# SwiGLU's second block products three positions later, in an attention, MoE and SwiGLU kernel on one core

## The chip, the cores and the metric

The kernel runs on one core of one Trainium2 chip. The metric is the device time of one execution in microseconds (us). The kernel before was timed in three runs: 2015.36 us median, 2013.31 to 2016.67.

## The reference

Three layers follow one another on 2304 tokens of width 512:

```
attention:  q_s = softmax over head_dim, k_s = softmax over seq, kv = k_s^T v, out = q_s kv
MoE:        P = 8 Sinkhorn rounds on exp(x w_gate); out = sum over 8 experts P[:, e] * (relu(x w1[e]) w2[e])
SwiGLU:     xn = x / rms(x) * g;  out = (silu(xn w_gate) * (xn w_val)) w_out
```

The expert products are 512 x 1024 x 512 for each of 8 experts, the SwiGLU products 512 x 1536 (twice) and 1536 x 512.

## The kernel before

**Groups and units.** The tokens lie in three groups of 512, 896 and 896 columns (groups 0, 1, 2). The hidden width is cut into chunks of 256. A unit is one chunk of one group: units 0 to 95 are the MoE, units 96 to 113 the SwiGLU: 96 to 101 (group 1), 102 to 107 (group 2), 108 to 113 (group 0). `NU` is 96, `NC2` 6 and `U0` 108. Every fp32 product is made of three fp32r matmuls on a high and a low part (`mm3`, lines 107 to 109).

**Seven block products.** For groups 1 and 2 the products are Strassen's: `seven` (line 856 on) makes seven products of 128 x 448 blocks, of six matmuls each, for the gate (`"a"`), then seven for the value (`"v"`). So a unit of 96 to 107 has fourteen positions, 0 to 13. After each product ScalarE copies or VectorE combines its PSUM bank (L873, L887, L891, L900, L901); there are two banks `b1`, one `b2`, one `b3`, so a later product waits for a bank that VectorE has not yet read. Then `later(i)` runs: Silu on ScalarE at positions 5 and 7, and one y tile.

**y tiles.** The second product of the gated chunk is also cut in seven blocks of two tiles: 14 y tiles of three matmuls (`yo`), which run one at each position of the unit after their own (`YS`, `y_step`). Tile p needs block p // 2 of the gated values (`SB`), and a quarter of the out-weights, wo block p // 4 (`WO`, 512 KB each, `wo_load`, L1194). VectorE adds a tile to its place from PSUM (L1284), or, for the four numbers in `STAGED`, ScalarE copies it out (L1281) and GpSimd adds it (L1282).

**Steps that make the gated blocks.** `tail_steps` gives nine: value(0) and value(1), products of 896 columns on VectorE (L1216), and seven blocks, each a cast on ScalarE (L103) and a subtraction on VectorE (L104); four of the steps also subtract on GpSimd (L1212). Before, they run at positions 11, 12, 13 of their unit and ahead of y tiles 0 to 5 of the next.

**Group 2's norm.** During units 97 to 100 `spread` hands out 59 steps that normalize group 2, transpose it and make seven sums for each of two halves. A sum is a cast on ScalarE (L392), a subtraction on VectorE (L395) and a store of both parts (L405, `sdB`, `sdT`); a piece of the store lies in one of two buffers, so a cast waits for the store of two sums ago. Before, places are positions 0 to 13 with 8 and 10 twice (16 in a unit).

**Queues.** All loads and stores here go out on SyncE's one queue in the order of the program. In unit u the gate weights of u + 1 are loaded after position 6 and the value weights of u + 1 after position 13 (`ws_load`, L300, two loads of 128 x 1792 fp32, for unit 102's value weights after its position 0). In unit 101, after positions 7 to 13, the seven sums of group 2 come back (`sx_load`, L808, 128 x 1792 fp32 each), each when its predecessor of group 1 has been used last. Before, wo blocks 0 to 3 of unit u are loaded after positions 3, 7, 11 and 13 of u; of unit 101 blocks 2 and 3 after positions 1 and 2 of unit 102.

**Units 108 to 113** are plain: four runs of matmuls (`plain`, gate twice, value twice, each of four steps kk of three matmuls over 512 columns); the y tiles of unit 107 run between the steps in unit 108. `w2_split` (L104 with L103) makes the parts of the out-weights of unit u after hooks 0 and 1 of u and then loads the next (`w2_load`, L188). Hooks 0 and 1 stand ahead of the gate runs, 2 behind them, 3 and 4 ahead of the value runs, 5 behind them. `y_end` and `y_store` (L1298, L1309) add and write out groups 1 and 2.

Of the kernel before, what the change touches and what calls it, by code (L numbers as in the profile page):

```python
# [18 lines left out]
def kernel(  # L19
# [34 lines left out]
    KD = DM // P  # L54
# [11 lines left out]
    NC2 = FF // CH  # L66
    NU = NG * NCH
# [5 lines left out]
    U0 = NU + 2 * NC2  # L73
# [28 lines left out]
    def split(hi, lo, src, eng=None):  # L102
        nc.scalar.copy(hi, src)  # L103
        (eng or nc.vector).tensor_tensor(lo, src, hi.bitcast(F32), op=ALU.subtract)  # L104
# [18 lines left out]
    def bank(kind, cols, name):  # L123
        turn = BANK[kind]
        turn.append(turn.pop(0))
        pool = turn[-1]
        if isinstance(pool, str):
            return pb_tile(pool, name)[:, :cols]
        return pool.tile([P, cols], F32, tag="p", name=name)
# [61 lines left out]
    def w2_split(u, f):  # L191
        rv = RAW["b", u]
        if f == 0:
            W2[u] = tuple(
                w2p.tile([P, 2, DM], F32R, tag=f"w2{w}", name=f"w2{w}_{u}") for w in "hl"
            )
        g = group(u)[0]
        if u < NU and g == 2:

            nc.scalar.copy(W2[u][0][:, f], rv[:, f])  # L200
            if f == 0:
                nc.sync.dma_start(
                    W2[u][1].rearrange("p f d -> p (f d)").bitcast(F32), W2D.pop(u)
                )
        else:
            split(W2[u][0][:, f], W2[u][1][:, f], rv[:, f])
        if f == 1:
            if u < NU and g == 1:
                W2D[u + NCH] = dram.tile([P, 2 * DM], F32, tag=f"w2l{u}", name=f"w2d_{u}")
                nc.sync.dma_start(  # L210
                    W2D[u + NCH], W2[u][1].rearrange("p f d -> p (f d)").bitcast(F32)
                )
            del RAW["b", u]
            if u + 1 != NU and u + 1 < ALL:
                w2_load(u + 1)
# [692 lines left out]
    def group(u):  # L908
        if u < NU:
            return divmod(u, NCH)  # L910
        j, c = divmod(u - NU, NC2)
        return TURN2[j], c
# [10 lines left out]
    def plain(u, f, key, stored):  # L923

        ph = bank("h", 2 * GP[0], f"ph_{key[0]}_{u}_{f}")
        if YS:
            for kk in range(KD):
                plain_mm(ph, f, key, stored, (kk,))
                y_step()
        else:  # L930
            plain_mm(ph, f, key, stored, range(KD))
        return ph

    def plain_mm(ph, f, key, stored, kks):
        wh, wl = WS[key]
        xh, xl = X0
        for kk in kks:
            if stored:
                i = ((2, 3), (0, 1))[f][kk // 2]
                lh, ll = wh[:, i, kk % 2], wl[:, i, kk % 2]  # L940
            else:
                lh, ll = (plain_view(t)[:, kk, f * P:(f + 1) * P] for t in (wh, wl))
            mm3(ph, lh, ll, xh[:, kk], xl[:, kk], kk == 0, kk == KD - 1)
# [189 lines left out]
    def unit2_h(u, hook):  # L1133
        g, c = group(u)
        n = 2 * GP[g]

        def gate_part(cf, to):
            nc.scalar.activation(to, cf, AF.Silu)

        def value_part(cf, to, f):  # L1140
            nc.vector.tensor_tensor(to, cf, to, op=ALU.mult)
            split(*h_tiles(u, f), to)

        cg = cp_.tile([P, 2, 2, G], F32, tag="c", name=f"cg_{u}")
        if g == 0:
            for f in range(2):
                hook(f)
                to = cg[:, f].rearrange("p t g -> p (t g)")[:, :n]
                gate_part(plain(u, f, ("a", u), True), to)
            del WS["a", u]  # L1150
            hook(2)
            for f in range(2):
                hook(3 + f)
                to = cg[:, f].rearrange("p t g -> p (t g)")[:, :n]
                value_part(plain(u, f, ("v", u), True), to, f)
            del WS["v", u]
            hook(5)
            return
        flat = lambda t, f: t[:, f].rearrange("p t g -> p (t g)")
        cv = cp2.tile([P, 2, 2, G], F32, tag="cv", name=f"cv_{u}")  # L1160
        mine = tail_steps(u, cg, cv)

        def later(i):
            if i in (5, 7):
                gate_part(flat(cg, i // 7), flat(cg, i // 7))
            elif i >= 11:
                mine.pop(0)()
            y_step()
            hook(i)

        hook(-1)
        seven(("a", u), cg, later, lambda f: None)
        seven(("v", u), cv, lambda i: later(7 + i), lambda f: None)
        assert not YS
        YS.extend(y_steps(u, mine))

    YS = []
    YM = {}
    SB = {}
    WO = {}  # L1180
    STAGED = (2, 4, 12, 13)
    OT = ["pch", "pcl"]

    def y_step():
        if YS:
            YS.pop(0)()
# [12 lines left out]
    def block(u, i, src):  # L1199

        tag = "h" + "hl"[i % 2] + "01"[i // 2 % 2]
        t = hp_.tile([P, 2 * G], F32R, tag=tag, name=f"s_{u}_{i}").rearrange(
            "p (w n) -> p w n", w=2
        )
        SB[u, i] = t
        split(t[:, 0], t[:, 1], src)

    def tail_steps(u, cg, cv):

        t1 = cp2.tile([P, G], F32, tag="t1", name=f"t1_{u}")  # L1210
        b11, b12, b21, b22 = (cv[:, f, t] for f in range(2) for t in range(2))
        sub = lambda o, x, y: nc.gpsimd.tensor_tensor(o, x, y, op=ALU.subtract)  # L1212
        row = lambda t, f: t[:, f].rearrange("p t g -> p (t g)")

        def value(f):
            nc.vector.tensor_tensor(row(cv, f), row(cv, f), row(cg, f), op=ALU.mult)  # L1216

        def s0():
            sub(t1, b12, b11)
            block(u, 0, b11)  # L1220

        def s1():
            block(u, 1, t1)

        def s2():
            value(1)

        def s3():
            block(u, 2, b21)
            sub(t1, b22, t1)  # L1230

        def s4():
            block(u, 3, t1)
            sub(b21, b21, t1)

        def s5():
            block(u, 4, b22)
            sub(b12, b22, b12)

        return [lambda: value(0), s0, s1, s2, s3, s4, s5, lambda: block(u, 5, b21), lambda: block(u, 6, b12)]  # L1240

    def ym_place(g):

# [12 lines left out]
        four = [big[:, n * 2 * G:(n + 1) * 2 * G] for n in range(4)]  # L1256
        YM[g] = four[:3] + [more_[0], four[3], more_[1], more_[2]]

    def y_steps(u, more_):

        g, c = group(u)

        def tile_(p):
            i, m = divmod(p, 2)
            if p == 0 and c == 0:
                ym_place(g)
            if more_:
                more_.pop(0)()
            py = bank("y", G, f"yo_{u}_{p}")
            w = WO[u, i // 2][:, i % 2, :, m * P:(m + 1) * P]  # L1270
            x = SB[u, i]
            mm3(py, w[:, 0], w[:, 1], x[:, 0], x[:, 1], True, True)
            a = YM[g][i][:, m * G:(m + 1) * G]
            if c == 0:
                if p % 2:
                    nc.vector.tensor_copy(a, py)
                else:
                    nc.scalar.copy(a, py)
            elif p in STAGED:
                t = accp.tile([P, G], F32, tag="yt", name=f"yt_{u}_{p}", bufs=2)  # L1280
                nc.scalar.copy(t, py)  # L1281
                nc.gpsimd.tensor_tensor(a, t, a, op=ALU.add)  # L1282
            else:
                nc.vector.tensor_tensor(a, py, a, op=ALU.add)  # L1284

        return [lambda p=p: tile_(p) for p in range(14)]
# [110 lines left out]
    def task(kind, u, i, fn):  # L1397
        TASK.setdefault((kind, u, i), []).append(fn)
# [4 lines left out]
    for n, key in enumerate(keys):  # L1403
# [3 lines left out]
        kd, u = keys[n - 2]  # L1407
        i = 6 if kd == "a" else 13
        if u >= NU and group(u)[0] == 0:
            i = 2 if kd == "a" else 5  # L1410
        at = {("v", NU): ("y", NU - 2, 0), ("v", NU + NC2): ("h", NU + NC2, 0)}
# [10 lines left out]
            task("h", u, 1 + f, lambda u=u, f=f: w2_split(u, f))  # L1422
    for u in range(U0, ALL):
        for f in range(2):
            task("h", u, 5 if u == U0 else f, lambda u=u, f=f: w2_split(u, f))
    for u in range(NU, U0):
        for i in range(4):
            at = ("h", u, min(4 * i + 3, 13))
            if u == NU:
                at = ("h", u, i) if i < 2 else ("y", u - 1, 6)  # L1430
            elif u == NU + NC2 - 1 and i > 1:
                at = ("h", u + 1, i - 1)
            task(*at, lambda u=u, i=i: wo_load(u, i))
    for u in range(NCH, 2 * NCH):
        task("h", u - 2, 2, lambda u=u: ws_sums(u))
# [96 lines left out]
    for i in range(7):  # L1532
        task("h", NU - 1, i, lambda i=i: sx_load(NG + 1, i))
        task("h", NU + NC2 - 1, 7 + i, lambda i=i: sx_load(NG + 2, i))
    spread(
        [("h", u, i) for u in range(NU + 1, NU + NC2 - 1) for i in (*range(14), 8, 10)],
        lambda: norm_steps(2),
    )
    spread(
# [11 lines left out]
    with tc.manual_schedule():  # L1551
# [59 lines left out]
        for step in START.split():  # L1611
            op, i = step.split("-")
# [68 lines left out]
        at = LATE * CPE  # L1681
# [6 lines left out]
        while n < len(order):  # L1688
            kind, u = order[n]
# [68 lines left out]
```

## Time and profile before

| | us |
|---|---|
| median of three runs | 2015.36 |
| the profiled execution | 2016.0 |
| its span, first to last instruction | 2013.9 |
| TensorE busy in the span | 1984.6 |
| VectorE busy | 1479.8 |
| ScalarE busy | 826.5 |
| GpSimd busy | 492.2 |

The profiled execution is 0.6 us above the median, and 2.1 us of it lie outside the span. Matmuls overlap in the records: one of 448 columns is shown with some 0.36 us, while the next starts 0.2 us later, so lost time is read from the starts and not from busy time. Times in the trace count from the span's start. The SwiGLU's units 96 to 107 lie between 1582 and 1901 us, the plain units behind them.

### The profile page before, as it was taken

The numbers are of one execution on the slowest core, as the hardware profiler recorded it, in microseconds if no ns is written. First come the engines' busy times: TensorE is split into PE (matmuls) and PEld (weight loads), VectorE is DVE, ScalarE is ACT, GpSimd is POOL, SyncE is SP. The second block draws the span as 40 slices with busy tenths as digits, with TensorE's granted clock in tenths as the row PEclk, the third lists the DMA queues.
The fourth block names the chain that finished last, engine by engine and source line by source line (L and its number), as shares of the span: only waits on it lengthen the run. The fifth ranks groups of instructions, "written<-read, shape, count | busy, mean of one in ns | idle before, by whom it ended". The sixth has DMA issues, their size and how long they took to land.

```text
span 2013.9 us, 26582 instructions
## 1 busy us (share of the span) xinstructions
PE 1984.6 (99%) x9614; PEld 1715.8 (85%) x9614; DVE 1479.8 (73%) x2382; ACT 826.5 (41%) x1508; POOL 492.2 (24%) x438
## 2 busy tenths in 40 slices
PE   7999999999999999999999999999999999999999
PEld 5777888888888888888888888888888897899987
DVE  8885877676667777777658878888875459788864
ACT  5564433345343334433244343443332274444421
POOL 3330000032222222222013332333320025433400
PEclk8999999999999999999999999999999999999999
DMA  8543232354755566654778888888875758867644
GB/s 199 141 143 105 94 101 95 96 199 182 271 204 195 203 220 222 210 198 177 297 264 285 283 278 315 306 303 307 314 273 177 275 201 279 338 227 249 244 167 143
DMA packets 192259, 441.90 MB, mean 219 GB/s; under 512 B 33920, under 2 KB 101504, under 8 KB 191744
## 3 DMA queue, kind: packets, MB, share of 16 engines
q1 hardware_dynamic: 188432, 438.38, 63.0%
q10 hardware_dynamic: 3696, 1.84, 0.3%
q8 instruction: 75, 1.23, 0.3%
q14 instruction: 56, 0.46, 0.1%
HBM read 297.42 MB, written 142.74 MB: 219 GB/s over the span
## 4 chain that ended last, share of the span: by engine, by line
PE 93%; DVE 4%; DMA 2%; ACT 1%; issue 0%; SPq 0%; DVEq 0%; ACTq 0%
PE py L107 13%; PE py L108 13%; PE py L109 13%; PE b_a L109 10%; PE b_a L107 10%; PE b_a L108 10%; PE ph_a L107 3%; PE ph_a L109 3%; PE ph_a L108 3%; PE b_v L109 1%; PE b_v L107 1%; PE b_v L108 1%; PE yo L107 1%; PE yo L108 1%; PE yo L109 1%; DMA wsl_v<-wdl_v 1%
## 5 line engine op out<-in xcount | busy, mean ns | idle before, releaser
L107 PE MATMUL py<-w2h,hh 128*128 128x512 f32 x1152 | 452.6, 393 | 0.7 <-ACT lt L751 0.7
L108 PE MATMUL py<-w2l,hh 128*128 128x512 f32 x1152 | 449.0, 390 | 0.0
L109 PE MATMUL py<-w2h,hl 128*128 128x512 f32 x1152 | 448.7, 389 | 0.0
L873 ACT COPY u_a<-b_a 128x448 f32<-128x448 f32 x228 | 121.6, 533 | 605.5 <-PE b_a L109 599.1
L107 PEld LDWEIGHTS py<-w2h,hh 128*128 128x128 f32 x1152 | 216.3, 188 | 47.2 <-issue 1.5
L109 PEld LDWEIGHTS py<-w2h,hl 128*128 128x128 f32 x1152 | 216.3, 188 | 45.8
L108 PEld LDWEIGHTS py<-w2l,hh 128*128 128x128 f32 x1152 | 216.4, 188 | 42.9
L107 PE MATMUL b_a<-sT,wsh_a 128*128 128x448 f32 x608 | 221.0, 364 | 2.4 <-DVE c L887 1.2
L109 PE MATMUL b_a<-sT,wsl_a 128*128 128x448 f32 x608 | 220.6, 363 | 0.0
L108 PE MATMUL b_a<-sT,wsh_a 128*128 128x448 f32 x608 | 220.5, 363 | 0.0
L1013 DVE SCALAR_TENSOR_TENSOR slot_a<-py,Pm,slot_a 128x512 f32<-128x512 f32 x217 | 162.5, 749 | 52.4 <-PE py L109 50.3
L1013 DVE SCALAR_TENSOR_TENSOR slot_b<-py,Pm,slot_b 128x512 f32<-128x512 f32 x217 | 160.5, 744 | 19.5 <-PE py L109 18.9
L107 PE MATMUL b_a<-sB,wsh_a 128*128 128x448 f32 x456 | 165.6, 363 | 0.1
L109 PE MATMUL b_a<-sB,wsl_a 128*128 128x448 f32 x456 | 165.6, 363 | 0.0
L108 PE MATMUL b_a<-sB,wsh_a 128*128 128x448 f32 x456 | 165.4, 363 | 0.0
L249 POOL TENSOR_TENSOR sum<-w1r 128x256 f32<-128x256 f32 x32 | 23.7, 740 | 561.5 <-PE ph_a L109 244.1
L898 POOL TENSOR_TENSOR c<-u_a,p_a 128x448 f32<-128x448 f32 x64 | 74.1, 1158 | 328.0 <-ACT u_a L873 311.2
L947 DVE SCALAR_TENSOR_TENSOR hl<-c,hh 128x896 fp32r<-128x896 f32 x128 | 143.5, 1121 | 0.9 <-ACT hh L946 0.7
L104 DVE TENSOR_TENSOR w2l<-w2r,w2h 128x512 fp32r<-128x512 f32 x138 | 100.1, 726 | 50.6 <-ACT w2h L103 50.5
L946 ACT ACTIVATE hh<-c 128x896 fp32r<-128x896 f32 x128 | 122.3, 956 | 29.4 <-POOL c L898 27.8
L107 PEld LDWEIGHTS b_a<-sT,wsh_a 128*128 128x128 f32 x608 | 113.8, 187 | 13.8 <-DVE c L887 2.4
L897 DVE TENSOR_TENSOR c<-b_a,u_a 128x448 f32<-128x448 f32 x64 | 39.9, 624 | 114.1 <-ACT u_a L873 114.1
(275 smaller groups left out, 3913.4 us busy)
## 6 DMA issues: line engine op xcount, KB each, us to landing
w2r<-in_moe_w_dram SPq DMA_DIRECT2D x96, 512.0 KB
w1r<-in_moe_w_dram SPq DMA_DIRECT2D x64, 512.0 KB
wsdh<-wsh_a SPq DMA_DIRECT2D x32, 896.0 KB
wsdl<-wsl_a SPq DMA_DIRECT2D x32, 896.0 KB
wsh_a<-wsdh SPq DMA_DIRECT2D x32, 896.0 KB
wsl_a<-wsdl SPq DMA_DIRECT2D x32, 896.0 KB
wo<-wd_o SPq DMA_DIRECT2D x36, 512.0 KB
w2d<-w2l SPq DMA_DIRECT2D x32, 512.0 KB
```

Source lines behind the costliest of these rows:

```text
L104: (eng or nc.vector).tensor_tensor(lo, src, hi.bitcast(F32), op=ALU.subtract)
L107: nc.tensor.matmul(ps, lh, rh, start=first, stop=False, skip_group_check=True)
L108: nc.tensor.matmul(ps, lh, rl, start=False, stop=False, skip_group_check=True)
L109: nc.tensor.matmul(ps, ll, rh, start=False, stop=last, skip_group_check=True)
L249: nc.gpsimd.tensor_tensor(s1, a21, a22, op=ALU.add)
L873: nc.scalar.copy(tmp[n], bk[i])
L897: nc.vector.tensor_tensor(c[:, 1, 0], bk[2], tmp["u3"], op=ALU.add)
L898: nc.gpsimd.tensor_tensor(c[:, 1, 1], tmp["u3"], tmp["p5"], op=ALU.add)
L946: nc.scalar.activation(th, src, AF.Relu)
L947: return lambda: nc.vector.scalar_tensor_tensor(tl, src, 0.0, th.bitcast(F32), op0=ALU.max, op1=ALU.subtract)
L1013: nc.vector.scalar_tensor_tensor(a, py, pe, a, op0=ALU.mult, op1=ALU.add)
```

## The change

The y tiles run three positions later: `YS` is filled up with empty steps to three ahead of a unit's fourteen, so tile p of unit u comes at position p + 3 of unit u + 1, and tiles 11 to 13 at positions 0 to 2 of unit u + 2. In unit 102 positions 0 to 6 take two tiles each. The nine steps get positions of their own through a table `MORE`: 11, 12, 13 of their unit and 0, 1, 3, 5, 7, 8 of the next (for unit 101's: 0, 0, 1, 2, 3, 4), ahead of that position's y tile. `STAGED` becomes 3, 8, 10, 11. The wo blocks move to positions 6 and 10 of their unit and 0 and 2 of the next, with exceptions at the ends of the groups: blocks 1, 2, 3 of unit 101 come after positions 1, 2, 3 of unit 102. The norm steps of group 2 get 15 places in a unit. In the plain units the parts of the out-weights are made three hooks later.

```diff
--- before.py
+++ after.py
@@ -923,12 +923,12 @@
     def plain(u, f, key, stored):
 
         ph = bank("h", 2 * GP[0], f"ph_{key[0]}_{u}_{f}")
-        if YS:
-            for kk in range(KD):
-                plain_mm(ph, f, key, stored, (kk,))
-                y_step()
-        else:
-            plain_mm(ph, f, key, stored, range(KD))
+        for kk in range(KD):
+            plain_mm(ph, f, key, stored, (kk,))
+            at = KD * (2 * (key[0] == "v") + f) + kk
+            for fn in MORE.pop((u, at), ()):
+                fn()
+            y_step()
         return ph
 
     def plain_mm(ph, f, key, stored, kks):
@@ -1158,27 +1158,30 @@
             return
         flat = lambda t, f: t[:, f].rearrange("p t g -> p (t g)")
         cv = cp2.tile([P, 2, 2, G], F32, tag="cv", name=f"cv_{u}")
-        mine = tail_steps(u, cg, cv)
+        tail_steps(u, cg, cv)
 
         def later(i):
             if i in (5, 7):
                 gate_part(flat(cg, i // 7), flat(cg, i // 7))
-            elif i >= 11:
-                mine.pop(0)()
+            for fn in MORE.pop((u, i), ()):
+                fn()
             y_step()
+            if u == NU + NC2 and i < 7:
+                y_step()
             hook(i)
 
         hook(-1)
         seven(("a", u), cg, later, lambda f: None)
         seven(("v", u), cv, lambda i: later(7 + i), lambda f: None)
-        assert not YS
-        YS.extend(y_steps(u, mine))
+        YS.extend([lambda: None] * max(0, LAG - len(YS)) + y_steps(u))
 
     YS = []
     YM = {}
     SB = {}
     WO = {}
-    STAGED = (2, 4, 12, 13)
+    STAGED = (3, 8, 10, 11)
+    LAG = 3
+    MORE = {}
     OT = ["pch", "pcl"]
 
     def y_step():
@@ -1219,9 +1222,6 @@
             sub(t1, b12, b11)
             block(u, 0, b11)
 
-        def s1():
-            block(u, 1, t1)
-
         def s2():
             value(1)
 
@@ -1237,7 +1237,13 @@
             block(u, 4, b22)
             sub(b12, b22, b12)
 
-        return [lambda: value(0), s0, s1, s2, s3, s4, s5, lambda: block(u, 5, b21), lambda: block(u, 6, b12)]
+        for i, fn in (
+            (11, lambda: value(0)), (12, s0), (13, lambda: block(u, 1, t1)), (14, s2), (15, s3),
+            (17, s4), (19, s5), (21, lambda: block(u, 5, b21)), (22, lambda: block(u, 6, b12)),
+        ):
+            if u == NU + NC2 - 1 and i > 14:
+                i = {15: 14, 17: 15, 19: 16, 21: 17, 22: 18}[i]
+            MORE.setdefault((u + i // 14, i % 14), []).append(fn)
 
     def ym_place(g):
 
@@ -1256,7 +1262,7 @@
         four = [big[:, n * 2 * G:(n + 1) * 2 * G] for n in range(4)]
         YM[g] = four[:3] + [more_[0], four[3], more_[1], more_[2]]
 
-    def y_steps(u, more_):
+    def y_steps(u):
 
         g, c = group(u)
 
@@ -1264,8 +1270,6 @@
             i, m = divmod(p, 2)
             if p == 0 and c == 0:
                 ym_place(g)
-            if more_:
-                more_.pop(0)()
             py = bank("y", G, f"yo_{u}_{p}")
             w = WO[u, i // 2][:, i % 2, :, m * P:(m + 1) * P]
             x = SB[u, i]
@@ -1422,14 +1426,18 @@
             task("h", u, 1 + f, lambda u=u, f=f: w2_split(u, f))
     for u in range(U0, ALL):
         for f in range(2):
-            task("h", u, 5 if u == U0 else f, lambda u=u, f=f: w2_split(u, f))
+            task("h", u, 5 if u == U0 else 3 + f, lambda u=u, f=f: w2_split(u, f))
     for u in range(NU, U0):
         for i in range(4):
-            at = ("h", u, min(4 * i + 3, 13))
+            at = (("h", u, 6), ("h", u, 10), ("h", u + 1, 0), ("h", u + 1, 2))[i]
             if u == NU:
                 at = ("h", u, i) if i < 2 else ("y", u - 1, 6)
-            elif u == NU + NC2 - 1 and i > 1:
-                at = ("h", u + 1, i - 1)
+            elif u == NU + NC2 - 1 and i > 0:
+                at = ("h", u + 1, i)
+            elif u == NU + NC2:
+                at = ("h", u, 8 + i)
+            elif u == U0 - 1 and i > 1:
+                at = ("h", u + 1, 1)
             task(*at, lambda u=u, i=i: wo_load(u, i))
     for u in range(NCH, 2 * NCH):
         task("h", u - 2, 2, lambda u=u: ws_sums(u))
@@ -1533,7 +1541,8 @@
         task("h", NU - 1, i, lambda i=i: sx_load(NG + 1, i))
         task("h", NU + NC2 - 1, 7 + i, lambda i=i: sx_load(NG + 2, i))
     spread(
-        [("h", u, i) for u in range(NU + 1, NU + NC2 - 1) for i in (*range(14), 8, 10)],
+        [("h", u, i) for u in range(NU + 1, NU + NC2 - 1) 
+         for i in (0, 1, 2, 4, 6, 8, 8, 9, 9, 10, 10, 10, 12, 13, 13)],
         lambda: norm_steps(2),
     )
     spread(
```

## Rows read from the trace of the kernel before

**Rows 1.** The page, its first part: TensorE's and the other engines' busy time.

```profile
PE 1984.6 (99%) x9614; PEld 1715.8 (85%) x9614; DVE 1479.8 (73%) x2382; ACT 826.5 (41%) x1508; POOL 492.2 (24%) x438
```

**Rows 2.** Windows of units 99, 100, 101, 102, 103: stretch, length, each engine's busy time.

```profile
1662.40:1691.40 29.00, 26.62 (x127) 23.29 (x126) 24.83 (x35) 14.37 (x29) 14.88 (x11) 1.00 0.85 290
1691.40:1720.20 28.80, 26.66 (x127) 23.23 (x127) 26.96 (x34) 14.08 (x28) 16.89 (x13) 1.00 0.85 279
1720.20:1745.70 25.50, 25.50 (x127) 23.65 (x127) 18.93 (x27) 11.65 (x22) 11.04 (x9) 1.00 0.79 291
1745.70:1773.90 28.20, 26.44 (x128) 23.35 (x128) 18.92 (x27) 11.63 (x22) 10.69 (x9) 1.00 0.89 357
1773.90:1799.30 25.40, 25.40 (x128) 23.68 (x127) 22.40 (x29) 13.31 (x26) 7.19 (x6) 1.00 0.63 217
```

**Rows 3.** TensorE's waits from 1575 us on: total us, times, longest.

```profile
PE b_v L107 <- DVE cg L901: 2.6, 2, 1.5
PE b_v L109 <- DMA wsl_v<-wdl_v: 1.5, 1, 1.5
PE b_a L107 <- DVE cg L887: 1.0, 2, 0.8
PE yo L108 <- DVE s L104: 0.8, 2, 0.6
```

**Rows 4.** VectorE's timeline, 1654 to 1683 us: start, length, instruction, idle before.

```profile
1660.74 0.62 DVE L395 TENSOR_TENSOR pcl_B<-slot_b,pch_B 128x448 fp32r<-128x448 f32 x1 [3.00 <-DMA sdB<-pcl_B]
...
1673.57 1.58 DVE L395 TENSOR_TENSOR pcl_T<-slot_b,pch_T 128x448 fp32r<-128x448 f32 x1
1675.08 1.57 DVE L104 TENSOR_TENSOR s<-cv,s 128x448 fp32r<-128x448 f32 x1
...
1680.27 0.62 DVE L395 TENSOR_TENSOR pcl_T<-slot_b,pch_T 128x448 fp32r<-128x448 f32 x1
...
1681.33 0.61 DVE L901 TENSOR_TENSOR cg<-b_a,u_a 128x448 f32<-128x448 f32 x1
```

**Rows 5.** GpSimd's timeline in the same stretch.

```profile
1673.12 1.55 POOL L1282 TENSOR_TENSOR slot_a<-yt,slot_a 128x448 f32<-128x448 f32 x1
1674.63 1.54 POOL L1212 TENSOR_TENSOR cv<-cv 128x448 f32<-128x448 f32 x1
```

**Rows 6.** SyncE's timeline, the loads it issues around the start of unit 102.

```profile
1732.35 0.32 SPq L300 DMA_DIRECT2D wsh_a<-wdh_a  x1
...
1734.99 0.32 SPq L1194 DMA_DIRECT2D wo<-wd_o  x1
...
1743.47 2.14 SPq L808 DMA_DIRECT2D sT<-sdT  x2
1745.66 0.42 SPq L300 DMA_DIRECT2D wsh_v<-wdh_v  x1
1746.14 0.42 SPq L300 DMA_DIRECT2D wsl_v<-wdl_v  x1
1746.60 2.11 SPq L1194 DMA_DIRECT2D wo<-wd_o  x2
```

**Rows 7.** Windows ahead of and during that backlog; last: TensorE's clock, DMA share, GB/s.

```profile
1727.00:1733.00 6.00, 6.00 (x32) 5.55 (x31) 4.33 (x7) 3.80 (x7) 4.64 (x4) 1.00 0.30 87
1733.00:1760.00 27.00, 26.73 (x129) 23.57 (x127) 19.63 (x29) 11.77 (x22) 10.68 (x8) 1.00 1.00 400
```

**Rows 8.** TensorE's timeline in unit 102.

```profile
1761.49 0.48 PE L109 MATMUL b_v<-sB,wsl_v 128*128 128x448 f32 x1 [1.54 <-DMA wsl_v<-wdl_v]
```

**Rows 9.** Windows early in the span; the third number from the end is TensorE's clock.

```profile
20.20:23.70 3.50, 2.01 (x34) 1.60 (x32) 3.40 (x9) 2.27 (x9) 2.15 (x2) 1.00 1.03 267
23.70:33.90 10.20, 9.68 (x49) 7.28 (x50) 9.21 (x20) 7.05 (x20) 3.72 (x3) 0.50 0.86 201
```

**Rows 10.** TensorE's timeline in units 109 and 112.

```profile
1927.28 0.50 PE L109 MATMUL ph_v<-slot_a,wsl_v 128*128 128x512 f32 x1 [0.47 <-DMA wsl_v<-wdl_v]
...
1971.32 0.50 PE L109 MATMUL ph_a<-slot_a,wsl_a 128*128 128x512 f32 x1 [0.21 <-DMA wsl_a<-wdl_a]
```

**Rows 11.** SyncE's timeline in unit 111.

```profile
1962.63 0.32 SPq L188 DMA_DIRECT2D w2r<-w  x1
1963.05 0.37 SPq L302 DMA_DIRECT2D wsh_a<-wdh_a  x1
```

## The prediction

> **What bounds the kernel now.** First the page's busy times: TensorE is busy for 1984.6 us of a span of 2013.9 [rows 1], so at most 29 us could be won by waiting less, in all stages together. The change adds and removes no matmul; it can only move waits. So I went to the stretch that it touches, unit by unit [rows 2]. Units 101 and 103 take 25.5 and 25.4 us with TensorE never idle; a unit is 14 positions of 9 matmuls, so one matmul starts every 25.4 / 126 = 0.202 us and a position takes 1.81 us. Against 25.4 us unit 99 loses 3.6, unit 100 3.4 and unit 102 2.8 us. That is what can be won here: 7.0 and 2.8 us.
>
> Then TensorE's waits [rows 3]. Those of units 99 and 100 end with VectorE: a product waits for a PSUM bank that VectorE reads late (L901, L887), and a y tile for a block made just ahead of it (L104). The idle times add up to less than the 7.0 us, since a stopped chain of matmuls also starts more slowly. The loss in unit 102 ends with a load of value weights.
>
> Why VectorE is late is in its timeline: it stands for 3.00 us on the store of a sum two before (its buffer is not free), and later subtractions on two SBUF operands take 1.57 us where the same one takes 0.62 at other times [rows 4]; the long ones lie beside GpSimd's own work [rows 5]. With that VectorE is busy for 24.8 of 29.0 and 27.0 of 28.8 us [rows 2].
>
> 0.2% of the time, about what a measurement of this kernel can tell from no change, is 4.0 us.
>
> **Part 1, y tiles later and block steps spread.** A block is now made five to seven positions ahead of its tile (9 us and more; three and four in unit 102), so the y tiles' wait on L104 goes. The steps no longer fall on six positions running (0 to 5); positions 2 and 4, where VectorE also evacuates products, are freed. So VectorE can catch up after position 1. It does as much as before, and GpSimd as well, so part of the long subtractions stays. The norm's places bring a new crowd: in unit 99 three sums fall on positions 8 to 10, in unit 100 three on 8 to 12. After position 6 SyncE issues weights and a wo block, 2.36 MB, 5.9 us at the 400 GB/s of a full queue [rows 7]; a store issued at position 8 stands behind them and lands around position 11, and the cast at position 10 needs its buffer. VectorE then stands for some 2 us (the nearest row shows 3.00 [rows 4]). Walking on from there with 0.53 us for an evacuation (two instructions from 1680.27 to 1681.33 [rows 4]), 1.0 for a value product, 1.1 to 1.6 for a subtraction beside GpSimd: the evacuation L901 of position 13 ends at about 28.2 us after the unit's start, and its bank is wanted at 16 x 1.81 = 29.0, in time by 0.8; at position 5 of the next unit a bank (L887) comes about 1 us late. I take 1.5 us that stay of the 7.0: **-5.5 us**. Bounds: all goes, -7.0; nothing goes, 0.
>
> **Part 2, the wo blocks of unit 101.** This is where a stall goes. The queue works in order and is full at the start of unit 102: from 1733 us on it moves 400 GB/s at a share of 1.00, after a slack stretch [rows 7]. What it has to carry is gate weights (2 x 0.917 MB), one wo block (0.524), seven sums (7 x 0.917) and value weights (2 x 0.917), 10.6 MB by their shapes; at 400 GB/s that is 26.4 us, and the last of the value weights, issued at 1746.14 [rows 6], lets a matmul start at 1761.49 [rows 8]. Before, wo block 1 of unit 101 is ahead of the sums, issued at 1734.99 [rows 6]. After, block 0 has that place, and block 1 is issued after position 1 of unit 102, so behind the value weights. It lands where block 2 stood: 0.524 MB at 400 GB/s is 1.3 us, so at 1761.4 + 1.3 = 1762.7, which is 17.0 us after the unit's start at 1745.7. It is needed by tile 4 of unit 101. Unit 102 takes three left-over tiles and then two at a position, so tile 4 is the eighth: it comes after 3 x 12 + 6 + 3 = 45 matmuls, 9.1 us into the unit. TensorE's queue is in order, so it waits there for 17.0 - 9.1 = **7.9 us**, and the seven products behind the tile with it. In return the old loss of 2.8 us goes: the last sums and the value weights have landed by then. Net **+5.1 us**. Bounds: -2.8 if the block is in time; +8.4 at the 357 GB/s that unit 102 has on average [rows 2], by which the 11.1 MB take 3.3 us more. Blocks 2 and 3 follow 1.3 us apart, ahead of their tiles. VectorE and ScalarE wait behind TensorE there, and lose nothing of their own.
>
> **Part 3, the clock after that wait.** Early in the span TensorE, busy for 2.01 of 3.50 us, is then shown at 0.50 of its 2.4 GHz for 10.2 us [rows 9], although it was busy for 9.68 us of them. No row shows a longer pause at full speed. So the price lies between 0 and half of 9.68, 4.8 us; no row is nearer to one end, and I take the middle, **+2.4 us**. The Trainium skill (TensorE: Matmul & The Clock Gate, section "Why this matters for your kernels") asks that long gaps between bursts of matmuls be avoided, because the clock then falls to half. It speaks against this change: by it the lower end drops out and the sum below lies between 2016.4 and 2018.8 us, without it it may be 2014.0. No row of the kernel before shows the rule after a gap of 8 us.
>
> **Part 4, the plain units.** Unit 109 now has one y tile ahead of its value run, which gives the value weights 0.6 us more; they were late by 0.47 [rows 10]. In unit 111 the gate weights' load stood in SyncE's queue behind the out-weights' load, which waits for VectorE, until 1963.05 [rows 11], and unit 112 waited 0.21 us for it [rows 10]. With the out-weights' steps three hooks later the gate weights go first, and the value weights come behind instead, which is the upper bound's case. With the slow restarts **-1.0 us**; bounds -1.5 and +1.0 (the value weights late by as much).
>
> **At nothing:** four tiles staged through ScalarE and GpSimd before and after. The plain runs keep their matmuls' order. Positions without a y tile (0 to 2 of unit 97, 10 to 13 of 102, 0 to 2 of 103) last 6 x 0.202 = 1.2 us; at 102's last four VectorE has 3.8 us of work (three evacuations of 0.53, a product of 1.0, two subtractions of 0.6) in 4.8, which hides it; without that cover a bank would be late by what is over. The norm's 59 steps end in unit 100 still, and the seven loads of sums start from the same place in unit 101.
>
> **The sum:** -5.5 + 5.1 + 2.4 - 1.0 = +1.0 us. The profiled execution, 2016.0, would be 2017.0; it lies 0.6 above the median, so I give 2015.4 + 1.0 = **2016.4 us**.
>
> **The rivals.**
> *The wo block is in time.* Should the queue let it pass the sums, or tile 4 come later than I count, parts 2 and 3 give only their gain: -5.5 - 2.8 - 1.0 = -9.3, 2006.1 us. For it: the change would then do all it can. Against it: the full queue up to 1760 us and the landing of the value weights 15 us after their issue [rows 6 to 8].
> *VectorE stays as late* (slower). Place: positions 8 to 13 of units 99 and 100; price: the 5.5 us are not won, so 5.1 + 2.4 - 1.0 = +6.5, 2021.9 us. It decides when the store of the first of the three sums lands later than about position 12: then L901's bank comes after position 2 of the next products, as before. For it: VectorE is busy for 27.0 us in unit 100 [rows 2], more than 25.4. Against it: its 34 instructions there, at 0.53 and two products at 1.0, make 19 us, so 8 us of the 27 are long subtractions, and positions behind the crowd are freed.
> *The clock holds* (the page's rule fails): -5.5 + 5.1 - 1.0 = -1.4, 2014.0; or it costs all 4.8 us: 2018.8. Both are within 0.2%, and part of the forecast.
>
> **How the numbers follow.** The forecast, with the clock either way, 0.56; its own range is 2012 to 2020. The block in time 0.23, VectorE as late 0.21. Faster by over 0.2% (under 2011.4): the first rival and a little of the forecast, 0.24; slower (over 2019.4): 0.22; within: 0.54. The range reaches from 2005.0, which holds the first rival, to 2021.5, which leaves half of the second out.
>
> **What would show it.** Right: units 99 and 100 near 25.4 us plus 1.5 in all; TensorE idle for some 8 us ahead of tile 4 (a `yo` matmul) in unit 102, ended by a wo load; its clock at 0.50 just behind it; no wait at 1761's value weights. Wrong: no wait ahead of `yo` in unit 102; L887 and L901 still among TensorE's longest waits; waits for value weights in units 110 to 113.

## The result, and the profile after

The changed kernel takes 2031.44 us (median of 5 runs, 2029.46 to 2033.07), the kernel before 2015.36: a ratio of 1.0082 (1.0072 to 1.0093), so it is 16 us slower. The profiled execution takes 2032.55 us, its span is 2030.6 us.

The page's first part and chain, after, beside [rows 1]:

```profile
PE 1987.7 (98%) x9614; PEld 1719.9 (85%) x9614; DVE 1473.8 (73%) x2382; ACT 825.4 (41%) x1508; POOL 495.8 (24%) x438
...
PE 91%; DVE 4%; DMA 3%; ACT 1%; issue 0%; POOL 0%; SPq 0%; ACTq 0%; DVEq 0%
```

The instructions are the same and busy times nearly so; only waiting was added. Windows of units 98, 99, 100, 101 and 102 (length, busy times, and third from the end TensorE's clock), beside [rows 2]:

```profile
1631.50:1661.60 30.10, 28.91 (x156) 26.57 (x155) 19.66 (x31) 20.58 (x42) 9.04 (x8) 1.00 0.60 211
1661.60:1688.30 26.70, 25.57 (x127) 23.51 (x126) 21.91 (x29) 12.84 (x25) 13.02 (x11) 1.00 0.84 284
1688.30:1718.30 30.00, 26.01 (x129) 23.57 (x128) 26.43 (x35) 12.94 (x25) 14.19 (x11) 1.00 0.81 266
1718.30:1750.80 32.50, 28.82 (x128) 25.84 (x127) 19.97 (x30) 13.10 (x25) 13.58 (x10) 0.89 0.71 262
1750.80:1788.90 38.10, 29.69 (x137) 27.09 (x136) 19.81 (x28) 11.72 (x23) 11.98 (x11) 0.87 0.72 284
```

Unit 99 is better than before (26.7 against 29.0 us), unit 100 worse, and unit 101, which lost nothing before, takes 32.5 instead of 25.5 us. Unit 102 with its 17 tiles has 135 matmuls, which need 27.3 us at 0.202 each, and takes 38.1. In units 101 and 102 the mean clock is below 1.00.

For a table by stretch the starts of successive matmuls are set against the regular pace, 0.20 us at 448 columns and 0.23 at 512; what lies above it is lost:

| lost, us | units 97-101 | 102 | 103-107 | 108-113 | span |
|---|---|---|---|---|---|
| before | 7.3 | 2.8 | 0 | 1.5 | 2013.9 |
| after | 14.9 | 10.8 | 0.5 | 2.4 | 2030.6 |

The differences, 7.6 + 8.0 + 0.5 + 0.9 = 17.0 us, are, but for rounding and the rest of the span, the 16.7 us by which the span grew. By unit, 98 to 101 lost 0.3, 3.6, 3.3 and 0 us before, and 1.9, 1.4, 4.5 and 7.1 after. TensorE's waits from 1570 us on, after, beside [rows 3]:

```profile
PE yo L107 <- DMA wo<-wd_o: 8.4, 1, 8.4
PE b_a L107 <- DVE cv L901: 5.1, 2, 3.4
PE b_a L107 <- DVE cg L887: 3.4, 2, 2.2
PE pn L1099 <- DVE slot_a L1288: 1.2, 2, 0.8
PE ph_v L109 <- DMA wsl_v<-wdl_v: 1.0, 1, 1.0
PE ph_v L107 <- DMA wsh_v<-wdh_v: 0.8, 1, 0.8
```

The wait of the y tiles on L104 is gone, the banks' waits have grown, and one wait for a wo block is the longest of the kernel. TensorE's timeline there, and SyncE's, beside [rows 6, 8]:

```profile
1759.72 0.37 PE L109 MATMUL yo<-s,wo 128*128 128x448 f32 x1
1768.50 0.71 PE L107 MATMUL yo<-s,wo 128*128 128x448 f32 x1 [8.41 <-DMA wo<-wd_o]
1769.01 0.57 PE L108 MATMUL yo<-s,wo 128*128 128x448 f32 x1
```

```profile
1738.31 0.38 SPq L1197 DMA_DIRECT2D wo<-wd_o  x1
...
1751.21 0.42 SPq L300 DMA_DIRECT2D wsl_v<-wdl_v  x1
1751.80 4.72 SPq L1197 DMA_DIRECT2D wo<-wd_o  x3
```

Block 1 is issued at 1751.80, behind the value weights, and lets tile 4 start at 1768.50, 17.7 us after the unit's start at 1750.8. Behind the wait matmuls stand at 0.57 us instead of 0.37, and start 0.37 us apart instead of 0.20. Windows around the two stretches at half clock (0.50 of 2.4 GHz), beside [rows 9]:

```profile
1725.40:1732.20 6.80, 6.20 (x17) 5.51 (x18) 5.20 (x8) 2.19 (x6) 6.18 (x5) 0.50 0.54 162
1732.20:1762.90 30.70, 27.89 (x138) 25.49 (x136) 22.59 (x33) 13.99 (x27) 13.00 (x10) 1.00 0.81 322
1762.90:1773.20 10.30, 4.70 (x13) 4.21 (x14) 1.59 (x3) 0.30 (x1) 0.00 (x0) 0.50 0.50 199
```

The other loss shows best in unit 101's start. ScalarE's timeline, then SyncE's, VectorE's and TensorE's:

```profile
1714.68 0.57 ACT L392 CAST pch_T<-slot_b 128x448 fp32r<-128x448 f32 x1 [1.72 <-DMA sdT<-pch_T]
1720.70 0.57 ACT L392 CAST pch_T<-slot_b 128x448 fp32r<-128x448 f32 x1 [5.46 <-DMA sdT<-pch_T]
1721.17 0.53 ACT L1285 COPY yt<-yo 128x448 f32<-128x448 f32 x1
1721.59 0.57 ACT L103 CAST s<-cv 128x448 fp32r<-128x448 f32 x1
```

```profile
1713.02 0.32 SPq L1197 DMA_DIRECT2D wo<-wd_o  x1
1713.43 0.39 SPq L405 DMA_DIRECT2D sdT<-pch_T  x1
```

```profile
1716.47 1.09 DVE L1219 TENSOR_TENSOR cv<-cv,cg 128x896 f32<-128x896 f32 x1
1722.19 1.21 DVE L104 TENSOR_TENSOR s<-cv,s 128x448 fp32r<-128x448 f32 x1 [4.64 <-ACT s L103]
...
1725.34 0.61 DVE L901 TENSOR_TENSOR cv<-b_v,u_v 128x448 f32<-128x448 f32 x1
```

```profile
1726.00 0.74 PE L107 MATMUL b_a<-sB,wsh_a 128*128 128x448 f32 x1 [3.38 <-DVE cv L901]
```

The last sum's cast waits 5.46 us on ScalarE for the store of the sum two before, which was issued at 1713.43 behind a wo block (1713.02). In ScalarE's order the cast of a gated block comes after it, VectorE's subtraction needs that, and so VectorE stands for 4.64 us, the evacuation L901 ends late, TensorE waits 3.38 us, and then runs at half clock.

### The profile page after: what moved, and what is told of

It reads as the page before. It is cut to its first block, busy times and chain, and to the rows that moved or that the text cites. A ratio compares the mean times of both kernels' runs of the same rounds, so it can differ in the third digit from the quotient of the medians.

```text
span 2030.6 us, 26572 instructions
## 1 busy us (share of the span) xinstructions
PE 1987.7 (98%) x9614; PEld 1719.9 (85%) x9614; DVE 1473.8 (73%) x2382; ACT 825.4 (41%) x1508; POOL 495.8 (24%) x438
## 4 chain that ended last, share of the span: by engine, by line
PE 91%; DVE 4%; DMA 3%; ACT 1%; issue 0%; POOL 0%; SPq 0%; ACTq 0%; DVEq 0%
PE py L107 13%; PE py L108 13%; PE py L109 13%; PE b_a L109 10%; PE b_a L107 10%; PE b_a L108 10%; PE ph_a L107 3%; PE ph_a L108 3%; PE ph_a L109 3%; PE yo L107 1%; PE yo L108 1%; PE yo L109 1%; PE b_v L107 1%; PE b_v L108 1%; PE b_v L109 1%; DMA wo<-wd_o 1%
## 5 line engine op out<-in xcount | busy, mean ns | idle before, releaser
L104 DVE TENSOR_TENSOR w2l<-w2r,w2h 128x512 fp32r<-128x512 f32 x138 | 100.0, 725 | 53.8 <-ACT w2h L103 53.8
```

## The experiments

All ran against the kernel before, on one chip in each group. The table gives each one's losses by stretch from its profile, as above; units 103 to 107 lose 0 to 0.9 us everywhere.

| lost, us | units 97-101 | 102 | 108-113 | span |
|---|---|---|---|---|
| a1_wo101 | 10.6 | 6.2 | 3.3 | 2023.3 |
| a2_norm | 7.0 | 10.3 | 2.1 | 2021.5 |
| a3_steps | 10.9 | 10.3 | 3.1 | 2025.7 |
| a4_staged | 9.2 | 10.5 | 2.7 | 2024.2 |
| b1_wofix_w2 | 12.4 | 1.3 | 0.5 | 2015.8 |
| b2_four | 3.7 | 1.5 | 2.5 | 2009.6 |
| b3_norm | 8.3 | 1.4 | 1.5 | 2013.0 |
| b4_norm_four | 4.9 | 1.1 | 0.1 | 2008.8 |
| c1_before_four | 2.6 | 2.8 | 2.2 | 2009.3 |
| c2_hooks | 3.6 | 1.4 | 0.6 | 2007.5 |
| d1_seven | 2.6 | 1.2 | 0.0 | 2005.8 |

The changed kernel, a1 and b1 are the same code in units 97 to 101 and lose 14.9, 10.6 and 12.4 us there: one profile of this stretch is good to some 2 us either way. b1 to b4 are the same code in units 108 to 113 and lose 0.5, 2.5, 1.5 and 0.1 us there.

**One block in time (a1).**

```diff
-            elif u == NU + NC2 - 1 and i > 0:
+            elif u == NU + NC2 - 1 and i > 1:
```

> The changed kernel with one thing undone: wo block 1 of unit 101 is loaded after position 10 of unit 101, ahead of the last sums, instead of after position 1 of unit 102. Theory (the block stood behind 9 MB in a queue that works in order): the wait of 8.4 us ahead of a y tile in unit 102 goes whole, and with it the half clock behind it, which cost 2.8 us by the matmuls' starts; together about 11 us less than the changed kernel, so 2020 us; the waits on VectorE in units 98 to 101 stay as they are (about 14 us with the half clock there). Rival (the two tiles at a position need the sums and weights themselves sooner than they come): the wait moves to the sums or the value weights of unit 102 and under 5 us are won.

Measured: 2027.39 us, 1.0068 (1.0051 to 1.0085) of before, and 6.2 us lost in unit 102 instead of 10.8. The time is 4 us below the changed kernel's, as little as the rival said, but for a reason that neither named: the wait of 8.4 us went, and the next block, still behind the value weights, now stops tile 8:

```profile
PE yo L107 <- DMA wo<-wd_o: 4.4, 1, 4.4
```

**One part undone at a time (a2, a3, a4)**: the norm's places, the block steps' positions, the staged tiles.

```diff
-        [("h", u, i) for u in range(NU + 1, NU + NC2 - 1) 
-         for i in (0, 1, 2, 4, 6, 8, 8, 9, 9, 10, 10, 10, 12, 13, 13)],
+        [("h", u, i) for u in range(NU + 1, NU + NC2 - 1) for i in (*range(14), 8, 10)],
```
```diff
-            (17, s4), (19, s5), (21, lambda: block(u, 5, b21)), (22, lambda: block(u, 6, b12)),
+            (16, s4), (17, s5), (18, lambda: block(u, 5, b21)), (19, lambda: block(u, 6, b12)),
...
```
```diff
-    STAGED = (3, 8, 10, 11)
+    STAGED = (2, 4, 12, 13)
```

> The changed kernel with the norm's steps of group 2 back at the places of before (each position once, 8 and 10 twice). Theory (the crowd of sums at positions 8 to 10 of unit 99 and 8 to 12 of unit 100 makes ScalarE and VectorE wait for stores, 5.46 and 2.90 us at the longest, and this makes the evacuations late): the waits of 3.4 and 2.2 us on L901 and L887 go below 1.5 us each and the clock stays at full speed in unit 101; 6 to 10 us less than the changed kernel, near 2023. Rival (the new positions of the block steps or of the staged tiles do it): under 3 us less.

> The changed kernel with the block steps back at six positions running (0 to 5 of the next unit), the y tiles still three later. Theory (the sums' places are to blame): the time stays within 3 us of the changed kernel's, 2031, or gets longer by 1 to 3, since VectorE is fuller at positions 0 to 5. Rival (the spread steps are to blame, value(1) at position 0 beside GpSimd's adds at 2.04 us for example): 4 us less or better.

> The changed kernel with the staged tiles back at numbers 2, 4, 12, 13, so that ScalarE's copies and GpSimd's adds come at positions 5, 7, 1 and 2 instead of 6, 11, 13 and 0. Theory (the sums' places are to blame): within 3 us of 2031; VectorE takes tiles 8, 10, 11 at positions 11, 13 and 0 and is later there by 0.5 us each. Rival (GpSimd's adds at 11, 13 and 0 lie beside the subtractions and make them long): long subtractions of 1.5 us become fewer at positions 12 to 1 and 4 us or more are won.

Measured in one run each: 2023.25, 2027.71 and 2026.18 us. With the norm's places of before the stretch loses 7.0 us, below all three profiles of the changed code there; as expected, the sums' places carry a good part of the loss. The waits did not all go below 1.5 us: two of 1.8 and 1.7 are left, on other banks, and the first halved the clock. The other two lose 10.9 and 9.2 us. Their times are 3.7 and 5.3 us below the changed kernel's, more than the 3 us expected. But one run says little (a1's four lie between 2025.29 and 2031.85), and 10.9 and 9.2 are too near the spread of 10.6 to 14.9 to call either a cause.

**Loads in the order of need (b1).** Blocks 1 and 2 of unit 101 ahead of unit 102's value weights, and the out-weights' steps back, but for unit 109:

```diff
-        at = {("v", NU): ("y", NU - 2, 0), ("v", NU + NC2): ("h", NU + NC2, 0)}
+        at = {("v", NU): ("y", NU - 2, 0), ("v", NU + NC2): ("h", NU + NC2, 2)}
...
-            task("h", u, 5 if u == U0 else 3 + f, lambda u=u, f=f: w2_split(u, f))
+            task("h", u, 5 if u == U0 else 3 + f if u == U0 + 1 else f, lambda u=u, f=f: w2_split(u, f))
...
-            elif u == NU + NC2 - 1 and i > 0:
-                at = ("h", u + 1, i)
+            elif u == NU + NC2 - 1 and i > 1:
+                at = ("h", u + 1, 2 * i - 3)
```

> The changed kernel with two things mended: wo blocks 1 and 2 of unit 101 are loaded after position 10 of unit 101 and after position 1 of unit 102, with unit 102's value weights behind them (after position 2), and in the plain units the out-weights' parts are made after hooks 0 and 1 again (in unit 109 still three later). Theory (a block that stands behind weights in the queue in order is late, in unit 102 and in the plain units alike): unit 102 loses under 1 us (changed kernel 10.8, with block 1 alone mended 6.2) and the plain units 1.5 or less (2.4 to 3.3); with 10 to 15 us still lost in units 97 to 101 the time is 2016 to 2021. Rival (two tiles at a position are too much for the loads however they are ordered): unit 102 still loses 3 us or more, to the value weights this time.

Measured: 2019.05 us, 1.0022 (1.0012 to 1.0031). Unit 102 loses 1.3 us, a little over the 1 us expected, and the plain units 0.5, so the theory holds for unit 102: a block is late by what stands ahead of it. Units 97 to 101 still lose 12.4.

**Four pieces (b2), the norm's places (b3), both (b4).** A sum on its way to its store lies in one of four places instead of two; two of them are tiles that lie idle until unit 102.

```diff
+    WIDE = [0]
+
+    def wide(name):
+        WIDE[0] += 1
+        if WIDE[0] % 4 < 2:
+            return piece(name)
+        t = accp.tile([P, 2 * G], F32, tag=f"x{WIDE[0] % 2 + 1}", name=f"pw_{name}")
+        return t[:, :G].bitcast(F32R), t[:, G:].bitcast(F32R)
...
-                    None if g == NG + 2 else staged, g == NG + 2,
+                    wide if g == NG + 2 else staged, g == NG + 2,
```

> The kernel with the two mends, and four pieces instead of two for group 2's sums on their way to the store (two of them in tiles that lie idle until unit 102). Theory (ScalarE's casts and VectorE's subtractions wait for the store of two sums ago, which stands behind weights in the queue, and everything behind them on both engines is late): units 97 to 101 lose under 4 us instead of 10 to 15; 2009 to 2012 us. Rival (VectorE is late because its subtractions run beside GpSimd, at 1.5 us instead of 0.6): 7 us or more are still lost there, 2015 or longer.

> The kernel with the two mends and the norm's steps at the places of before, two pieces. Theory: units 97 to 101 lose about 7 us, as with these places before (7.3 before the change, 7.0 with the rest of the change), so 2012 to 2015 us: the spread block steps and later y tiles win nothing there. Rival (they win something once the half clock and the late blocks are out of the way): under 4 us lost, 2010.

> The two mends, the norm's places of before, and four pieces. Theory (stores): units 97 to 101 lose under 2 us, 2007 to 2010 us, faster than both kernels. Rival (GpSimd beside VectorE): 5 us or more are still lost, 2012 or longer.

Measured: b2 2010.63 us, 0.9972 (0.9963 to 0.9982); b3 2014.88, 0.9997 (0.9988 to 1.0006); b4 2011.97, 0.9982 (0.9973 to 0.9992). Four pieces alone take units 97 to 101 from 12.4 to 3.7 us, as the theory said. ScalarE's waits for stores, in b1,

```profile
ACT pch_T L392 <- DMA sdT<-pch_T: 9.7, 3, 4.1
...
ACT pch_T L392 <- DMA sdB<-pch_B: 1.5, 2, 0.9
...
ACT pch_B L392 <- DMA sdB<-pch_B: 0.9, 1, 0.9
```

have no counterpart in b2, where TensorE's longest waits in the SwiGLU are

```profile
PE ph_a L109 <- DMA wsl_a<-wdl_a: 1.9, 2, 1.3
PE b_a L107 <- DVE cg L895: 1.5, 1, 1.5
PE pn L1107 <- DVE slot_a L1296: 1.2, 2, 0.8
```

(lines are 8 further on here). With two pieces and the norm's places of before, b3, the rest of the change is as fast as the kernel before; its spread steps and later tiles win nothing in units 97 to 101 (8.3 against 7.3 us). With four pieces the places matter less (3.7 and 4.9).

b4 missed its forecast: 4.9 us lost instead of under 2, next to its rival's 5. ScalarE, VectorE and GpSimd wait for no store in its units 97 to 101, and yet in unit 99 TensorE waits for an evacuation, and falls to half clock at 1679.9 us. Ahead of that wait VectorE has instructions that run long beside GpSimd's:

```profile
1663.22 1.59 DVE L403 TENSOR_TENSOR pcl_T<-slot_b,pch_T 128x448 fp32r<-128x448 f32 x1
1664.73 2.05 DVE L1227 TENSOR_TENSOR cv<-cv,cg 128x896 f32<-128x896 f32 x1
```

```profile
1678.71 0.47 PE L107 MATMUL b_v<-sB,wsh_v 128*128 128x448 f32 x1 [1.79 <-DVE cg L909]
```

So with the stores out of the way VectorE's own work can still make it late; how much of that the long instructions carry was not tried.

**Four pieces without the change (c1)**, the same edit on the kernel before.

> The kernel before with four pieces for group 2's sums, nothing else of the change. Theory (the waits for stores make VectorE late, before the change as behind it): units 97 to 101 lose 3 us or less instead of 7.3, so about 2011 us; unit 102 keeps its 2.8 us. Rival (before the change it is the six block steps running that make VectorE late): 5 us or more are still lost, 2013 to 2015.

Measured: 2011.67 us, 0.998 (0.9971 to 0.9989); units 97 to 101 lose 2.6 instead of 7.3 us. Windows of units 99 and 100, beside [rows 2], and two of VectorE's subtractions:

```profile
1661.70:1688.10 26.40, 25.74 (x127) 23.58 (x127) 24.61 (x34) 14.15 (x28) 14.75 (x12) 1.00 0.93 312
1688.10:1714.90 26.80, 25.72 (x128) 23.58 (x127) 25.12 (x32) 13.11 (x26) 15.34 (x12) 1.00 0.92 310
```

```profile
1670.51 1.58 DVE L403 TENSOR_TENSOR pcl_T<-slot_b,pch_T 128x448 fp32r<-128x448 f32 x1
1672.02 1.57 DVE L104 TENSOR_TENSOR s<-cv,s 128x448 fp32r<-128x448 f32 x1
```

ScalarE's waits for stores in units 97 to 101 were, before,

```profile
ACT pch_B L392 <- DMA sdT<-pch_T: 4.0, 2, 3.4
ACT pch_B L392 <- DMA sdB<-pch_B: 3.1, 2, 2.2
...
ACT pch_T L392 <- DMA sdT<-pch_T: 1.0, 1, 1.0
```

and in c1 one of 0.2 us is left. VectorE is still busy for 24.6 of 26.4 us, and its subtractions are as long beside GpSimd as before [rows 4]. So the waits for stores carried 4.7 of the 7.3 us, and the long subtractions, which stayed, no more than the 2.6 that are left.

**The loads of the plain units (c2), and one place moved (d1).** c2 is the changed kernel with four pieces, b1's order in unit 102, and the out-weights' parts made after hooks 2 and 3, behind the gate weights' load and further ahead of the value weights':

```diff
-            task("h", u, 5 if u == U0 else 3 + f, lambda u=u, f=f: w2_split(u, f))
+            task("h", u, 5 if u == U0 else 3 + f if u == U0 + 1 else 2 + f, lambda u=u, f=f: w2_split(u, f))
```

d1 also has the norm's places `(0, 1, 2, 4, 6, 7, 8, ...)` instead of `(0, 1, 2, 4, 6, 8, 8, ...)`.

> The changed kernel with four pieces, wo blocks 1 and 2 of unit 101 ahead of unit 102's value weights, and the out-weights' parts of units 110 to 113 made after hooks 2 and 3, that is behind the load of the next gate weights and further ahead of the value weights' load than in the change. Theory (each load in the plain units is late by what waits ahead of it in SyncE's queue): the plain units lose under 1 us (2.4 to 3.3 with hooks 3 and 4, 0.1 to 2.5 with hooks 0 and 1), units 97 to 101 about 4, unit 102 under 1.5; 2008 to 2011 us, faster than both kernels. Rival (it is the number of stores beside them, wherever the parts are made): 2 us or more stay there.

> The kernel with four pieces, the wo blocks ahead of unit 102's value weights and the out-weights' parts after hooks 2 and 3, with one more place moved: the norm has places at positions 7 and 8 instead of twice 8. Theory (two transposes of group 2 behind one another need four banks of the y tiles at once, and the second waits for the tile just made): the waits of 0.8 and 0.4 us ahead of the transposes in unit 98 go, 1.3 us less than the kernel without this move (2009.25), so 2008 us. Rival (ScalarE, which empties the transposes' banks and makes a Silu at position 7, is the limit there): the wait only moves, and the time stays within 0.5 us.

Measured: c2 2009.25 us, 0.997 (0.996 to 0.9981), with 0.6 us lost in units 108 to 113, and 0.0 in d1. That is as forecast, but does not show that the order of the loads decides there: six profiles with hooks 0 and 1 lose 0.1 to 2.5 us, and c2's ratio is close to that of b2 (0.997 and 0.9972). With hooks 3 and 4, the changed kernel and a1 to a4, it is 2.1 to 3.3. d1 2007.99 us, **0.996 (0.9947 to 0.9972)**, the lowest of all, though its interval overlaps that of c2. Unit 98 takes 29.0 us instead of c2's 30.1, and of the two waits ahead of the transposes 0.3 us are left:

```profile
PE b_a L107 <- DVE cg L895: 1.5, 1, 1.5
PE b_v L109 <- DMA wsl_v<-wdl_v: 0.6, 1, 0.6
PE pn L1107 <- ACT slot_b L1114: 0.3, 1, 0.3
```

Against c1, the rest of the change as mended here wins 1.6 us in unit 102: the six profiles with blocks 1 and 2 both ahead of the value weights lose 1.1 to 1.5 us there, the kernel before and c1 2.8. It wins nothing in units 97 to 101, where both lose 2.6, and its 2.2 us in the plain units lie within the spread of one code there.

## Why the prediction was wrong

**The step that failed is part 1.** "-5.5 us. Bounds: all goes, -7.0; nothing goes, 0" was +7.6 in the profile. I saw the crowd of sums and the store behind it. Three things were wrong.

The walk from unit 99's crowd was too short. Unit 99 itself did get shorter, but the two banks at the end of the walk are wanted in unit 100. I had VectorE stand for some 2 us; first ScalarE stood for 2.90 us, then VectorE for 1.79. The evacuation L901 ended 32.2 us after the unit's start at 1661.6 instead of 28.2, and TensorE waited 1.74 us for it where I had 0.8 us to spare; L887 then cost 2.24 us instead of about 1:

```profile
1684.88 0.57 ACT L392 CAST pch_T<-slot_b 128x448 fp32r<-128x448 f32 x1 [2.90 <-DMA sdT<-pch_T]
```

```profile
1687.91 0.87 DVE L395 TENSOR_TENSOR pcl_B<-slot_b,pch_B 128x448 fp32r<-128x448 f32 x1 [1.79 <-DMA sdT<-pcl_T]
...
1693.21 0.60 DVE L901 TENSOR_TENSOR cv<-b_v,u_v 128x448 f32<-128x448 f32 x1
```

```profile
1693.87 0.47 PE L107 MATMUL b_a<-sB,wsh_a 128*128 128x448 f32 x1 [1.74 <-DVE cv L901]
...
1701.84 0.47 PE L107 MATMUL b_a<-sT,wsh_a 128*128 128x448 f32 x1 [2.24 <-DVE cg L887]
```

I did not walk unit 100, which gave the largest loss, 7.1 us in unit 101. Two casts fall on the same position there, 10. A store is issued only ahead of the next cast, so the second cast waits for the whole way of a store just issued, behind a wo block that the change moved to that very position: 5.46 us. ScalarE stands, and everything behind it in its order, the gated blocks' casts and the staged tile's copy, is late with it (VectorE then stood 4.64 us). b2 shows that these waits are the cause: with four pieces, and nothing else changed from b1, they are gone, and units 97 to 101 lose 3.7 us instead of 12.4.

And I took 0 as the upper bound. A place where a wait can be added has no such bound; the nearest row, 3.00 us for one store [rows 4], once in each of units 99 and 100 on top of what was lost before, would have given one above zero. The slower rival had the mechanism and the place, but only the price of nothing gained. The range ended 10 us short.

**Parts 2 and 3 held.** The wait ahead of tile 4 was 7.9 us forecast and 8.41 measured; the block landed 17.7 us after the unit's start, 17.0 forecast. The half clock behind it took 13 matmuls at 0.37 us, some 2.2 us, 2.4 forecast. The Trainium skill's advice on gaps (TensorE: Matmul & The Clock Gate, section "Why this matters for your kernels") agrees with this trace: 0.50 behind 8.41 us of idle. That part 3 came out so near was luck: I took the middle of a wide range, and of the 10.3 us at 0.50 the first 5.6 lay in the wait itself. The stretch at half clock of [rows 9], from which the range came, seems to have cost little: six profiles without one there reach unit 97 at 1606.8 to 1607.8 us, the kernel before at 1608.5. Together unit 102 lost 8.0 us more than before, 7.5 forecast. The rival that the block is in time fell. But I asked for the clock's price in one place, and it was also paid in unit 101, 2.9 us behind a wait of 3.38.

**Part 4** came out near its upper bound, +0.9 instead of -1.0, though one profile tells little there: unit 109's wait went, but in unit 112 the value weights now stand behind the out-weights' load, which waits for VectorE:

```profile
1991.76 0.47 PE L107 MATMUL ph_v<-slot_a,wsh_v 128*128 128x512 f32 x1 [0.83 <-DMA wsh_v<-wdh_v]
...
1993.47 0.50 PE L109 MATMUL ph_v<-slot_a,wsl_v 128*128 128x512 f32 x1 [1.00 <-DMA wsl_v<-wdl_v]
```

**At nothing**, the two transposes at position 8 of unit 98 were not in the sum; unit 98 takes 30.1 us instead of 28.5, 1.6 more, of which 1.2 are waits for VectorE ahead of the transposes; d1 won 1.1 back. That the y tiles' wait on L104 goes was right.

What stays open is how units 97 to 101 would do in many profiles; the split of their loss among the sums' places, the staged tiles and the block steps with two pieces rests on one profile each. Nor is it shown what makes up the 2.6 to 4.9 us that stay with four pieces.

## What to carry to other kernels

Before steps are moved on a busy engine, ask what it stands for: here VectorE looked overloaded, and what held it was ScalarE waiting for a buffer whose store stood in a queue behind weights; two more buffers won most of what the change was after (4.2 us, without it), and with two pieces no order of the steps tried here lost clearly less in units 97 to 101 than the order before. In a queue that works in order, place each load by when it is needed, and count what stands ahead of it in bytes. Where a moved step can add a wait, give its cost an upper bound above zero.

## What the runs showed of the hardware

TensorE's clock fell behind waits far shorter than 8.41 us, and not behind each. In units 97 to 101 a wait of 1.79 us (a2) was followed by 3.4 us at half clock, one of 1.75 (b3) was not. Behind a wait of 2.24 us the clock stayed at 1.00 in the changed kernel, behind one of 2.25 in a1, the same code there, it fell to 0.50; and behind one of 2.53 in a1 it stayed. Such a stretch at half clock costs up to half of its length, which was 3.4 us in a1 to a4, b1, b3 and b4 and 6.8 in the changed kernel, and may explain part of the spread between profiles of one code.
